# Reciprocals by GpSimd, moved small steps and a third tile of sign ranks in a fused attention and mixture-of-depths kernel

## The chip, the cores and the metric

The kernel runs on one core of one Trainium2 chip. The core has five engines that run at the same time, each with a queue of its own that it works through in order: TensorE (PE in the profile; its weight loads are shown apart as PEld), VectorE (DVE), ScalarE (ACT), GpSimd (POOL) and SyncE (SP), which issues most of the transfers. An engine waits for another by semaphores. The metric is the device time of one execution in microseconds, less is better, as the median of several executions.

## The reference

There are 8 batches, 8 heads, 576 rows of 64 channels. The first block is attention that keeps, in each row of scores, only the 32 largest:

```python
scores = scale * np.matmul(q, k.transpose(0, 1, 3, 2))
kth = np.partition(scores, -top_k, axis=-1)[..., -top_k:-top_k + 1]
scores = np.where(scores >= kth, scores, -1000000000.0)
scores = scores - np.max(scores, axis=-1, keepdims=True)
attn = np.exp(scores)
attn = attn / (np.sum(attn, axis=-1, keepdims=True) + 1e-09)
return np.matmul(attn, v)
```

Its heads are joined to rows of 512, and the second block, a mixture of depths, sends the 128 rows of each batch with the highest gate through a two-layer network:

```python
scores = np.einsum('bsd,d->bs', x, w_gate)
for b in range(B):
    top_idx = np.argpartition(-scores[b], capacity)[:capacity]
    xe = x[b, top_idx]
    ye = np.maximum(xe @ w1, 0.0) @ w2
    g = 1.0 / (1.0 + np.exp(-scores[b, top_idx]))
    out[b, top_idx] = x[b, top_idx] + g[:, None] * ye
```

## The kernel before

**Units.** A batch has five tiles of rows: four of 128 rows (tile numbers 0 to 3) and one of 64 (tile 4, `J`). A unit is one tile and two heads (for the last tile two heads of each half of the partitions), 18 units in a batch, 144 in all. The main loop (`for n in range(-1, N)`) is a software pipeline: in step n it multiplies the scores of unit n+1, searches the bound of unit n, finds the 32nd value of unit n-2, masks unit n-3 and forms the weighted values of unit n-4. `InOrder` keeps each engine's instructions in the order in which the program states them, so that the text of the loop is the order of every queue.

**One unit, engine by engine.**

- ScalarE copies the two score rows of 576 from PSUM (`keep`, tile `sc`).
- VectorE searches a bound (`find_bound`): for each of the two rows seven first maxima over a seventh of the row each (`cand`), then three rounds of eight maxima over the candidates, with the found ones struck out in between. The result is a bound that about the 24th largest score meets.
- ScalarE compares the row with that bound by a Sign (`part`, tiles `sides` in FP8 and the count `seen`), GpSimd multiplies the row by those signs and adds a short tail of fill values (`weigh_signs`, `fill`, tile `y`), and VectorE takes eight maxima of `y` (`find_kth`, tile `next`): the eighth is the 32nd largest score.
- ScalarE masks one row with it and GpSimd the other (`mask`, tile `less`).
- TensorE transposes the scores and adds the masks times a large negative number to them (`turn`, tile `ptr`). ScalarE takes the exponential (`pT`, `last`), TensorE multiplies by the values (`values`), with a column of ones that gives the sum of the weights.

**A finished tile.** After its last unit, ScalarE copies the products (`xs`) and the sums of weights (`keep_sums`, tile `sums`, eight numbers per row). One step later `normalise` calls `divide`: VectorE forms the eight reciprocals (`rden`), GpSimd multiplies. `normalise` is put on `vector_late`, a list that `find_bound` empties after the seven first maxima of its first row. Another step later VectorE forms the gates of the tile (`gates`, `dot`: a product with `wg` and a sum).

**The mixture of a batch** (`mixture`) is a generator whose pieces are spread over the steps of the next batch by the lists `mix_at` and `mix_at_of`. After the gates went through DRAM to a row on every partition (`gate_row`), the rank of each row of the batch is found tile by tile: for tiles 0 and 1 ScalarE adds up signs of gate differences (`weigh_gates`, put on `late`, which is emptied in each step ahead of the copies of the scores), for tiles 2, 3 and 4 VectorE counts larger gates (`choose`, on `vector_late`). GpSimd turns each rank into a row of the selection matrix `pick` (`choose_slot`, on `pool_late`, which is emptied after the bound of a step). TensorE then multiplies, and VectorE makes row numbers and gates of the products (`add_up`, on `after_kth`, emptied at the end of a step, behind the maxima of `y`). GpSimd fetches the chosen rows by an indirect transfer (`fetch_rows`), ScalarE forms exp(-gate), VectorE adds 1 and inverts (`squash`, on `vector_late`), TensorE runs the two layers, ScalarE scales the result by the gate, and GpSimd adds it to the output by another indirect transfer. For the last batch the same is written out by hand after the loop, with ranks counted in parts.

**A check at the end.** For each batch `keep_least` keeps the smallest 32nd value (`least`, a reduction by VectorE over 36 numbers a row) and a copy of the bounds. The last stage tests these, the counts and the sums; if a test fails, a slower general branch computes everything again. It isn't taken in these runs.

All instructions of the loop go through one recording line, so the profile gives L46 for them; they are told apart by the names of their tiles.

Of the kernel before, what the change touches and what calls it, by code (L numbers as in the profile page):

```python
# [11 lines left out]
ALU = mybir.AluOpType  # L12
FP32 = mybir.dt.float32
BF16 = mybir.dt.bfloat16
FP8 = mybir.dt.float8e4
# [34 lines left out]
def kernel(  # L50
# [11 lines left out]
    nc = tc.nc  # L62
    P = nc.NUM_PARTITIONS
    B, H, S, D = q.shape
# [55 lines left out]
    for i in range(2):  # L120
# [23 lines left out]
    bounded = const.tile([P, NS], FP32, name="bounded")  # L144
    sums = const.tile([P, B * NT, H], FP32, name="sums")
    nc.gpsimd.memset(sums, 1.0)

    MIDDLE = S - 2 * (TOP_K - 8) + 1
    steps_i = const.tile([P, 2, 8], I32, name="steps_i")
# [8 lines left out]
    nc.gpsimd.memset(ranks, 0.0)  # L158


    signs = const.tile([P, B - 1, 2], FP32, name="signs")
    places = const.tile([P, B, 7], FP32, name="places")
    nc.gpsimd.memset(places, 1.0)
    slot_signs = const.tile([P, CAP], FP32, name="slot_signs")
# [1 line left out]
        out=slot_signs,  # L166
# [57 lines left out]

    kept, values_bank = [], [None]

    after_kth = []

    def flush_copies():
        while copies_late:  # L230
# [2 lines left out]
    def flush():  # L233
        flush_copies()
        while late:
            late.pop(0)()
# [307 lines left out]
    def find_bound(sc, bound):  # L544

        cand = wkpool.tile([P, 2, 8 * PARTS], FP32, name="cand")
        best = [stats.tile([P, 2, 8], FP32, name=f"best{r}") for r in range(2)]
        best.append(bound)
        for i in range(2):

            if i == 1:
                flush_vector()
            for u in range(PARTS):
                if (i, u) == (1, 2) and amid_late:
                    amid_late.pop()()
                dve.max(
                    cand[:, i, 8 * u : 8 * u + 8],
                    sc[:, i, u * S // PARTS : (u + 1) * S // PARTS],
                )


        parts = cand.rearrange("p i (u e) -> p i u e", u=PARTS)
        for r, e in enumerate((3, 7, 8)):
            for i in range(2):
                dve.max(best[r][:, i, :], parts[:, i, :, 0:e])
            if r < 2:
                for i in range(2):
                    dve.match_replace(
                        parts[:, i, :, 0:e],
                        best[r][:, i, :],  # L570
                        parts[:, i, :, 0:e],
                        LOWEST,
                    )
# [163 lines left out]

    def divide(n, xs, x, den):
        rden = stats.tile([P, H], FP32, name="rden")
        dve.reciprocal(out=rden[0:n, :], in_=den)  # L740
        pool.tensor_tensor(
            x.rearrange("p (h d) -> p h d", h=H),
            xs[0:n, :, 0:D],
            rden[0:n, :].unsqueeze(2).to_broadcast([n, H, D]),
            ALU.mult,
        )
# [39 lines left out]
    def mixture(row0, pg, rank, exact=False, sign_sum=None):  # L786
# [36 lines left out]
        def choose_slot(t, n, slot=slot, rank=None):  # L823
            if rank is None:
                rank = rank_of[:, t : t + 1]
            pool.tensor_scalar(
                out=pick[0:n, t, :],
                in0=slot[0:n, :],
                scalar1=rank[0:n, :],
                scalar2=None,  # L830
                op0=ALU.is_equal,
            )

        for t in range(NT):
            yield
            n = R if t == J else P


            def weigh_gates(t=t):
                total = sign_sum[:, t : t + 1]  # L840
                act.activation(
                    pick.rearrange("p t c -> p (t c)")[:, 0:S],
                    gate_row,
                    AF.Sign,
                    bias=gate[:, t : t + 1],
                    scale=-1.0,
                    accum_out=total,
                )
                if t == 1:
                    for u in range(2):  # L850
                        pool_late.append(
                            lambda u=u: choose_slot(
                                u, P, slot_signs, sign_sum[:, u : u + 1]
                            )
                        )

            if t < 2 and not exact:
                late.append(weigh_gates)
                continue

            def choose(t=t, n=n):
                junk = modpool.tile([P, S], FP32, name="junk", tag="scratch")
                dve.tensor_scalar(
                    out=junk[0:n, :],
                    in0=gate_row[0:n, :],
                    scalar1=gate[0:n, t : t + 1],
                    scalar2=None,
                    op0=ALU.is_gt,
                    op1=ALU.add,
                    accum_out=rank[0:n, t : t + 1],  # L870
                )
                if exact:
                    break_ties(t, gate, gate_row, rank)

                pool_late.append(lambda: choose_slot(t, n))

            vector_late.append(choose)
# [16 lines left out]

        def add_up():
            add_parts(place, found)
            keep_rows(
                place,
                row_i,
                row0 if isinstance(row0, float) else row0[:, 0:1],  # L900
                float(done * S - 1),
            )
            dve.tensor_scalar_max(out=g, in0=place[:, 1:2], scalar1=-88.0)
            late.append(lambda: act.activation(g, g, AF.Exp, scale=-1.0))

        def squash():
            dve.tensor_scalar_add(out=g, in0=g, scalar1=1.0)
            dve.reciprocal(out=g, in_=g)

        kept.append(lambda: after_kth.append(add_up))  # L910
        if exact:
            for todo in (kept, after_kth):
                while todo:
                    todo.pop(0)()
        yield
# [15 lines left out]
        for fc in range(NFC):  # L931
            yield
            if fc == 1:
                vector_late.append(squash)
            if fc % 2 == 0:
                ps = ps_misc.tile([P, 2, CAP], FP32, name="h_ps", tag="misc")
            multiply_h(ps[:, fc % 2, :], fc, xeT)
            if fc % 2 == 1:
                copies_late.append(
                    lambda ps=ps, fc=fc: act.activation(  # L940
                        hT[:, fc - 1 : fc + 1, :], ps, AF.Relu
                    )
                )
# [34 lines left out]
    def add_parts(place, found):  # L978
        dve.tensor_reduce(
            out=place,  # L980
            in_=found[:, 0:6].rearrange("p (a e) -> p a e", e=3),
            axis=mybir.AxisListType.X,
            op=ALU.add,
        )

    def keep_rows(ps, row_i, row0, most):

        dve.tensor_scalar(
            out=row_i,
            in0=ps[:, 0:1],  # L990
            scalar1=row0,
            scalar2=most,
            op0=ALU.add,
            op1=ALU.min,
        )
# [178 lines left out]
    def keep_least(b, bound, kth):  # L1174
        at = 2 * per_batch * b
        late.append(
            lambda: act.copy(
                out=bounded[:, at : at + 2 * per_batch].rearrange("p (n i) -> p n i", i=2),
                in_=bound,
            )  # L1180
        )
        dve.tensor_reduce(
            out=least[:, b : b + 1], in_=kth, axis=mybir.AxisListType.XY, op=ALU.min
        )

    def mask_of(n, on=None):
# [346 lines left out]
        )  # L1533

    keep_least(B - 1, bounds.pop(B - 1)[:, :, :, 7], next8s.pop(B - 1)[:, :, :, 7])
    flush()
    low = modpool.tile([P, S], I32, name="low", tag="scratch")[:, 0:NS]
    dve.tensor_scalar(
# [88 lines left out]
    def general_weights(sc):  # L1627

        p = wkpool.tile([P, 2, S], FP32, name="p", tag="y")
        for i in range(2):  # L1630
            cur, tops = sc[:, i, :], []
            left = wkpool.tile([P, 2, S], FP32, name="left", tag="y")
            for r in range(TOP_K // 8):
                tops.append(stats.tile([P, 8], FP32, name=f"top{r}", bufs=2))
                nc.vector.max(tops[-1], cur)
                if r < TOP_K // 8 - 1:
                    nc.vector.match_replace(left[:, 0, :], tops[-1], cur, LOWEST)
                    cur = left[:, 0, :]
            shift = stats.tile([P, 1], FP32, name="shift", bufs=2)
            nc.vector.tensor_scalar_mul(shift, tops[0][:, 0:1], -scale)  # L1640
            e = wkpool.tile([P, S], FP32, name="e", tag="sides")
            nc.scalar.activation(
                e, sc[:, i, :], AF.Exp, bias=shift, scale=scale
            )
            nc.vector.scalar_tensor_tensor(
                out=p[:, i, :],
                in0=sc[:, i, :],
                scalar=tops[-1][:, 7:8],
                in1=e,
                op0=ALU.is_ge,  # L1650
                op1=ALU.mult,
            )
        return p
# [77 lines left out]
```

## Time and profile before

| | |
|---|---|
| median of 3 runs | 786.59 us (786.38 to 789.53) |
| the profiled execution | 788.9 us |
| its span, first to last instruction | 786.6 us |
| busy: TensorE, VectorE, ScalarE, GpSimd | 725.7, 756.7, 731.3, 692.4 us |
| main loop, units of steady batches | 92.29 us a batch of 18 units |
| VectorE busy from 50 to 700 us | 49.85 to 50.00 of every 50 us |
| ScalarE busy from 50 to 700 us | 47.11 to 49.94 of every 50 us |
| GpSimd busy from 50 to 700 us | 45.97 to 47.54 of every 50 us |
| mean granted TensorE clock | 0.996 of full speed |

In the profile a group of instructions stands in one row: line, engine, operation, what it writes and reads, shapes, count; then after the bar the busy time in microseconds and the mean of one in nanoseconds; then the idle time of the engine just before them, with the engine and tile whose semaphore ended most of it. In a list in order of time a row has the start and the length in microseconds, and in square brackets an idle time ahead of it. On VectorE and ScalarE the next instruction starts before the recorded end of the one before, so the lengths add up to more than the time that passes; the distance from start to start is what an instruction takes of its engine.

### The profile page before, as it was taken

To read this page: it belongs to the slowest core of one execution; us is meant where nothing else is said; L and a number is where in the kernel's file an instruction comes from. 1 tells how busy PE (TensorE), PEld (TensorE's weight loads), DVE (VectorE), ACT (ScalarE), POOL (GpSimd) and SP (SyncE) were. 2 spreads that over 40 slices of the span, in tenths; PEclk is the share of its full clock that TensorE was granted. 3 is DMA by queue.
4 is the path that set the end of the run, shared out by engine and by line. 5 is a ranking of instruction groups with operands and counts; after the bars stand their busy time and mean duration, and the time that the engine had idled before them with its cause. 6 is when DMAs were issued, how large, how long until landed. Compare 5 with 4: busy or idle time off the path is not lost. (4 is left out here: it accounts for less than half of the span.)

```text
span 786.6 us, 33176 instructions
## 1 busy us (share of the span) xinstructions
PE 725.7 (92%) x12535; PEld 550.5 (70%) x12535; DVE 756.7 (96%) x4602; ACT 731.3 (93%) x1535; POOL 692.4 (88%) x732
## 2 busy tenths in 40 slices
PE   8888888888999989999999999999899989999987
PEld 6766666666786668766786667866687658757756
DVE  7999999999999999999999999999999999999952
ACT  6999999999999999999999999999999999989730
POOL 3899999999999998999999999999999999999821
PEclk9999999999999999999999999999999999999899
DMA  8941215121151132321251221512233102101021
GB/s 168 293 105 39 48 56 111 30 55 30 62 118 35 38 94 54 76 57 42 70 110 31 56 43 63 114 26 50 65 77 82 30 15 70 25 15 17 2 75 31
DMA packets 121751, 50.69 MB, mean 64 GB/s; under 512 B 116016, under 2 KB 116016, under 8 KB 120560
## 3 DMA queue, kind: packets, MB, share of 16 engines
q1 hardware_dynamic: 118368, 43.94, 22.7%
q0 software_dynamic: 1744, 4.20, 3.0%
q8 instruction: 101, 1.65, 0.9%
q14 instruction: 66, 0.54, 0.2%
q10 hardware_dynamic: 1472, 0.36, 0.2%
HBM read 36.93 MB, written 11.55 MB: 62 GB/s over the span
## 5 line engine op out<-in xcount | busy, mean ns | idle before, releaser
L46 POOL TENSOR_TENSOR y<-sc,sides 128x576 f32<-128x576 f32 x288 | 349.8, 1237 | 24.8 <-ACT sides L46 23.3
L46 DVE MAX8 cand<-sc 128x8 f32<-128x82 f32 (+1 forms) x2016 | 313.1, 230 | 3.0 <-ACT sc L46 2.9
L46 POOL TENSOR_SCALAR less<-sc,next 128x576 bf16<-128x576 f32 x135 | 233.3, 1728 | 28.4 <-DVE next L46 23.8
L46 ACT ACTIVATE sides<-sc,bound 128x576 fp8e4<-128x576 f32 x288 | 230.9, 802 | 3.9 <-DVE bound L46 3.7
L46 PEld LDWEIGHTS av<-v,pT 128*64 128x64 f32 x4608 | 146.9, 138 | 87.2 <-ACT last L46 78.7
L46 DVE MAX8 next<-y 128x8 f32<-128x584 f32 x288 | 204.4, 751 | 0.0
L46 PE MATMUL av<-v,pT 128*64 128x65 f32 x4608 | 166.9, 225 | 35.0 <-ACT last L46 34.7
L46 PE MATMUL ps<-kT,qT 64*128 64x288 f32 (+1 forms) x1248 | 170.4, 422 | 2.9 <-ACT sc L46 2.1
L46 PEld LDWEIGHTS <-less 64*128 64x128 bf16 (+1 forms) x2448 | 161.2, 131 | 13.0 <-POOL less L46 10.0
L46 PE MATMUL ptr<-ident,sc 64*128 64x64 f32 x2272 | 161.5, 253 | 0.0
L46 ACT COPY sc<-ps 128x1152 f32<-128x1152 f32 x140 | 160.5, 1146 | 0.0
L46 ACT ACTIVATE pT<-ptr 128x1024 f32<-128x1024 f32 x142 | 147.3, 1037 | 10.1 <-PE ptr L46 9.3
L46 PEld LDWEIGHTS ptr<-ident,sc 64*128 64x128 f32 x2272 | 138.2, 137 | 23.8 <-issue 23.7
L46 PE MATMUL ptr<-out_of_reach,less 64*128 64x64 bf16 x2272 | 148.2, 190 | 6.3 <-POOL less L46 5.3
L46 ACT ACTIVATE less<-sc,next 128x576 bf16<-128x576 f32 x147 | 115.4, 789 | 0.0
L46 PEld LDWEIGHTS ps<-kT,qT 64*128 64x128 f32 (+1 forms) x1248 | 92.6, 176 | 22.6 <-ACT sc L46 5.1
L46 DVE MATCH_REPLACE8 cand<-best,cand 128x21 f32<-128x21 f32 (+1 forms) x576 | 99.0, 180 | 0.0
L46 DVE MAX8 best<-cand 128x8 f32<-128x21 f32 (+1 forms) x576 | 91.0, 191 | 0.0
L46 ACT ACTIVATION_READ_ACCUMULATOR sides<-sc,bound 128x1 f32 x288 | 63.6, 221 | 0.0
L46 PE MATMUL h_ps<-xeT,w 128*128 128x128 f32 x464 | 61.9, 278 | 0.0
L46 PEld LDWEIGHTS av<-ident,sc 128*128 128x128 f32 x144 | 20.0, 139 | 55.9 <-issue 40.9
L46 PE MATMUL av<-vpair,last 128*64 128x130 f32 x576 | 56.9, 276 | 0.0
(167 smaller groups left out, 916.2 us busy)
## 6 DMA issues: line engine op xcount, KB each, us to landing
v<-in_v_dram SPq DMA_DIRECT2D x64, 128.0 KB, 4.0
out_dram<-x SPq DMA_DIRECT2D x8, 1024.0 KB, 3.9
rows<-in_k_dram SPq DMA_DIRECT2D x56, 128.0 KB, 2.9
rows<-in_q_dram SPq DMA_DIRECT2D x56, 128.0 KB, 3.1
w<-in_moe_w_dram SPq DMA_DIRECT2D x2, 2048.0 KB
gate_row<-row_dram SPq DMA_DIRECT2D x7, 288.0 KB, 4.6
last<-in_q_dram SPq DMA_DIRECT2D x8, 128.0 KB, 3.5
vpair<-in_v_dram SPq DMA_DIRECT2D x16, 64.0 KB, 5.1
```

The costliest lines, as they stand in the source:

```text
L46: return lambda *a, **kw: self._tc.keep_in_program_order(fn(*a, **kw))
```

## The change

The change has three parts and two consequences.

1. `divide` and `squash` form their reciprocals on GpSimd, as a power with exponent -1. A new constant tile `minus_one` holds the exponents. The addition of 1 in `squash` goes along, and `squash` is put on `pool_late`.
2. A new list `after_max` is emptied by `find_bound` after each first maximum, so in effect after the first one of the next unit. On it go the reduction of `least` and the part of `add_up` that follows its sum: `use_place`, with the row number, the limited gate and the request for its exponential.
3. `SIGNED` = 3 tiles, not two, have their ranks added up from signs by ScalarE. The signs are written to a tile of their own in FP8 (`gate_signs`) and not to `pick`, and each tile's slots are chosen as soon as its sum is there, not those of tiles 0 and 1 together.

In the general branch, a work tile takes another buffer. The last stage's own reciprocals, written out there, stay on VectorE.

```diff
+    minus_one = const.tile([P, H], FP32, name="minus_one")
+    nc.gpsimd.memset(minus_one, -1.0)
...
-    signs = const.tile([P, B - 1, 2], FP32, name="signs")
+    SIGNED = 3
+    signs = const.tile([P, B - 1, SIGNED], FP32, name="signs")
...
-    after_kth = []
+    after_kth, after_max = [], []
...
                 dve.max(
                     cand[:, i, 8 * u : 8 * u + 8],
                     sc[:, i, u * S // PARTS : (u + 1) * S // PARTS],
                 )
+                while after_max:
+                    after_max.pop(0)()
...
     def divide(n, xs, x, den):
         rden = stats.tile([P, H], FP32, name="rden")
-        dve.reciprocal(out=rden[0:n, :], in_=den)
+        pool.tensor_tensor(rden[0:n, :], den, minus_one[0:n, :], ALU.pow)
         pool.tensor_tensor(
             x.rearrange("p (h d) -> p h d", h=H),
             xs[0:n, :, 0:D],
...
             def weigh_gates(t=t):
                 total = sign_sum[:, t : t + 1]
+                unread = modpool.tile([P, S], FP8, name="gate_signs")
                 act.activation(
-                    pick.rearrange("p t c -> p (t c)")[:, 0:S],
+                    unread,
                     gate_row,
                     AF.Sign,
                     bias=gate[:, t : t + 1],
                     scale=-1.0,
                     accum_out=total,
+                    saturate=False,
                 )
-                if t == 1:
-                    for u in range(2):
-                        pool_late.append(
-                            lambda u=u: choose_slot(
-                                u, P, slot_signs, sign_sum[:, u : u + 1]
-                            )
-                        )
-
-            if t < 2 and not exact:
+                pool_late.append(lambda: choose_slot(t, P, slot_signs, total))
+
+            if t < SIGNED and not exact:
                 late.append(weigh_gates)
                 continue
...
         def add_up():
             add_parts(place, found)
+            after_max.append(use_place)
+
+        def use_place():
             keep_rows(
...
         def squash():
-            dve.tensor_scalar_add(out=g, in0=g, scalar1=1.0)
-            dve.reciprocal(out=g, in_=g)
+            pool.tensor_scalar(
+                out=g, in0=g, scalar1=1.0, scalar2=None, op0=ALU.add
+            )
+            pool.tensor_tensor(g, g, minus_one[:, 0:1], ALU.pow)

         kept.append(lambda: after_kth.append(add_up))
         if exact:
-            for todo in (kept, after_kth):
+            for todo in (kept, after_kth, after_max):
                 while todo:
                     todo.pop(0)()
...
             if fc == 1:
-                vector_late.append(squash)
+                pool_late.append(squash)
...
-        dve.tensor_reduce(
-            out=least[:, b : b + 1], in_=kth, axis=mybir.AxisListType.XY, op=ALU.min
+        after_max.append(
+            lambda: dve.tensor_reduce(
+                out=least[:, b : b + 1], in_=kth, axis=mybir.AxisListType.XY, op=ALU.min
+            )
         )
...
     keep_least(B - 1, bounds.pop(B - 1)[:, :, :, 7], next8s.pop(B - 1)[:, :, :, 7])
+    after_max.pop()()
     flush()
```

More of the change, by code (lines that the diff above doesn't have):

```diff
@@ L1640, in general_weights @@
             nc.vector.tensor_scalar_mul(shift, tops[0][:, 0:1], -scale)
-            e = wkpool.tile([P, S], FP32, name="e", tag="sides")
+            e = modpool.tile([P, S], FP32, name="e", tag="scratch")
             nc.scalar.activation(
```

## The prediction

> **What bounds the kernel now.** I read the page's busy table first, then the costliest groups, then one steady batch, then single stretches of each engine in order of time.
>
> ```profile
> PE 725.7 (92%) x12535; PEld 550.5 (70%) x12535; DVE 756.7 (96%) x4602; ACT 731.3 (93%) x1535; POOL 692.4 (88%) x732
> 381.69:473.98 92.29, 88.75 (x1549) 66.78 (x1549) 92.19 (x569) 91.27 (x194) 86.46 (x89) 1.00 0.27 63
> ```
>
> The second line is busy time in one batch of 18 units, from a unit's first maximum to the same one a batch later: PE, PEld, DVE, ACT, POOL. The batch before and the one after have the same period, 92.3 us. VectorE is never idle, ScalarE is idle 1.0 us, GpSimd 5.8 us. So VectorE sets the period, and ScalarE stands about 1% behind it: that second fact decides how much of a cut on VectorE can be cashed. What VectorE does beside its maxima:
>
> ```profile
> L46 DVE TENSOR_SCALAR_CACHE_REDUCE junk<-gate_row,gate 128x576 f32<-128x576 f32 x14 | 11.2, 799 | 0.0
> L46 DVE RECIPROCAL rden<-sums 128x8 f32<-128x8 f32 x32 | 6.0, 188 | 2.4 <-ACT sums L46 2.4
> L46 DVE RECIPROCAL g<-g 128x1 f32<-128x1 f32 x8 | 1.3, 164 | 0.3
> ```
>
> Durations overstate what an instruction costs its engine, because the next one starts before it ends. VectorE in order of time:
>
> ```profile
> 471.65 1.42 DVE L46 MAX8 next<-y 128x8 f32<-128x584 f32 x2
> 473.10 0.22 DVE L46 TENSOR_REDUCE least<-next 128x1 f32<-128x36 f32 x1
> 473.24 1.11 DVE L46 MAX8 cand<-sc 128x8 f32<-128x82 f32 x7
> 474.26 0.18 DVE L46 RECIPROCAL rden<-sums 128x8 f32<-128x8 f32 x1
> 474.37 0.34 DVE L46 MAX8 cand<-sc 128x8 f32<-128x82 f32 x2
> ```
>
> The reciprocal occupies 474.37 - 474.26 = 0.10 us (unrounded 0.101), not 0.188. The reduction starts 0.03 us after the maxima end instead of some 0.085 us before: it reads what they have just written, and VectorE stands still 0.12 us for it. The rank of one tile:
>
> ```profile
> 443.11 0.80 DVE L46 TENSOR_SCALAR_CACHE_REDUCE junk<-gate_row,gate 128x576 f32<-128x576 f32 x1
> 443.82 0.08 DVE L46 DVE_READ_ACCUMULATOR junk<-gate_row,gate 128x1 f32 x1
> 443.82 1.12 DVE L46 MAX8 cand<-sc 128x8 f32<-128x82 f32 x7
> ```
>
> occupies 0.72 us. The same rank as a sum of signs on ScalarE:
>
> ```profile
> 422.66 0.83 ACT L46 ACTIVATE pick<-gate_row,gate 128x576 bf16<-128x576 f32 x1
> 423.33 0.26 ACT L46 ACTIVATION_READ_ACCUMULATOR pick<-gate_row,gate 128x1 f32 x1
> 423.42 0.44 ACT L46 ACTIVATE qT<-ps 128x256 f32<-128x256 f32 x1
> ```
>
> occupies 423.42 - 422.66 = 0.76 us. On GpSimd, where a tile is normalised:
>
> ```profile
> 453.30 1.72 POOL L46 TENSOR_SCALAR less<-sc,next 128x576 bf16<-128x576 f32 x1 [0.65 <-DVE next L46]
> 455.00 1.03 POOL L46 TENSOR_TENSOR x<-xs,rden 128x512 f32<-128x512 f32 x1
> 456.00 2.39 POOL L46 TENSOR_TENSOR y<-sc,sides 128x576 f32<-128x576 f32 x2
> ```
>
> The multiply follows the mask at once; it doesn't wait for VectorE's reciprocal.
>
> **What the Trainium skill says.** "Perfetto Trace Analysis", GPSIMD Engine Instruction: GpSimd spans are unreliable, take start-to-start spacing. I do; the trace agrees where it matters (the mask: 1.72 long, 1.70 spaced). "ScalarE: Activation LUTs", What ACT_TABLE_LOAD costs: 280 ns + 0.833 ns an element with a pointer bias, back-to-back overlap about 93 ns. For 576 elements that is an estimate of 760 and 667; an unqueued Sign here takes 767, spaced 667. "GPSIMD Engine Reference", 3.1: about 2.6 cycles an element for two inputs, 1.25 us for 576 by its 1.2 GHz; the trace has 1237 ns. No page prices a power on GpSimd.
>
> **The change, part by part** (spacing, not duration).
> VectorE loses, over the run:
> - 38 reciprocals of the sums in the loop at 0.10 us: 3.8. (Of the 40 rows one is in the last stage through the same helper, one stays.)
> - Seven ranks of tile 2 at 0.72: 5.0.
> - Seven squashes (add, then a reciprocal that waits for it: 0.174 + 0.080): 1.8.
> - Seven reductions of the thresholds, moved behind the first maximum of the next unit: the stall of 0.12 each, 0.8. The instruction stays.
> - The row number and gate moved likewise: row_i started 0.034 us after the sum ended and now follows a maximum, 0.12 each, 0.8.
> Together 12.3 us, 1.76 per batch in steady state. The moved steps issue no DMA. What waits for them: the fetch of the rows by GpSimd comes after a 1.7 us mask that itself waits for the maxima, so a row number about 0.5 us later is covered (uncovered: 0.5 us seven times, on GpSimd); the Exp of the gate slips one unit, and its reader comes units later.
>
> ScalarE gains seven Signs at 0.76: 5.3. Each stands in its queue ahead of the copies of the turned rows and of the next scores, and so of everything VectorE reads next. The FP8 target instead of pick takes away a write that pick's readers had to release; ScalarE never waits visibly for that, so nothing.
>
> GpSimd gains 39 powers of 8 wide, seven adds and seven powers 1 wide. Slots chosen stay at 35; they come one by one. The mask or multiply that follows in GpSimd's queue waits behind each. A small operation that waits for its predecessor is spaced 0.27 us here (the splits of the gates, 200 ns each), the lower bound of a power. No row bounds it from above. A 576-element multiply spends about 1.8 ns an element; if a power is 20 to 40 of those, eight are 0.3 to 0.6 us: estimate 0.55 for the whole spacing, and I let it run to 1.5. New work per batch at 0.55: 5 x 0.55 + 0.27 + 0.4 = 3.4 us.
>
> **Why VectorE's 12.3 us won't all arrive.** I set each start-to-start spacing of ScalarE in the batch above against the shortest tenth of its kind. The excess that ends with another engine is about 1.6 us of 92.29: 0.7 waiting for the bounds from VectorE, 0.8 for turned scores from TensorE, 0.1 other. Give it 0.76 and take away every wait: 92.29 - 1.6 + 0.76 = 91.45. VectorE would need 92.29 - 1.76 = 90.53. ScalarE becomes the bound. The wait for the bounds disappears by itself (VectorE is early); the wait for TensorE only in part, since TensorE itself waits for ScalarE's last weights and for GpSimd's masks. I take 1.25 of 1.6 as removable: gain 0.5 per batch.
>
> The margin that VectorE can run ahead first: it starts a unit 1.3 to 3.8 us after that unit's scores are copied, 2.19 in the unit right after the new Sign. So:
> - up to the first wait for scores: 2.19 - 0.76 = 1.4 us
> - four further batches at 0.5: 2.0
> - the last batch, after the last such wait, where ScalarE has slack (busy 42.9 of the 50 us from 700 on): VectorE's own savings, 1.5
> - last stage: the last normalisation starts at 751.44 after sums ending 751.12; the power takes 0.3 us more than the reciprocal, and the values of the last unit queue behind the gates: -0.3. The two counts that stood behind VectorE's 2.4 us wait for those sums run earlier, but nothing waits for them there.
> Sum 4.6 us.
>
> The profiled execution took 788.9 us, with a span of 786.6, so 2.3 us lie around it; they don't change. The median of the runs is 786.59. I take the difference off the median: 782.0 us.
>
> **Rivals.**
> - *VectorE stays the bound.* All of 12.3: 774.3 us. For it: VectorE has no idle, and parts of ScalarE's spacing may shrink when less queues. Against: the 1 us of idle. 0.17.
> - *ScalarE sets the pace*, 782.0, itself 779 to 784.5. 0.45.
> - *The gain is absorbed.* GpSimd's mask is ready between 0.5 us before and 0.9 us after TensorE starts that unit's turns, and ScalarE takes the result as little as 0.07 us later. Powers ahead of masks make those later by their length in the units where GpSimd has no idle (30 us at a time), so ScalarE's waits stay: gain 0 to 0.1 per batch, 785.5. That the change doesn't do what it says belongs here. 0.18.
> - *GpSimd becomes the bound* (slower). Its spacings, taken the same way, fill 85.3 of 92.29 us. With powers of p in both widths it needs 85.3 + 6p + 0.27; above p = 1.1 us that exceeds today's period. At 1.4: 94.0, 1.7 a batch, seven batches: 798 us. 0.20.
>
> **How the numbers follow.** A measurement of this kernel tells about 0.5% from no change, so 782.66 and 790.5 are the edges. Faster: 0.17 and four fifths of 0.45, 0.53. Same: the other fifth and 0.18, 0.27. Slower 0.20. The range runs from the full VectorE gain, 774, to 790, which holds the absorbed case and a power just above its threshold; most of the slower case is left out.
>
> **What would show it.** VectorE: waits for the score copies on the first maximum, 0 to 1 us in the units after the new Sign, where there were none; its busy time 12 to 17 us less. ScalarE: its waits for the bounds gone, its busy share of a steady batch over 99%. GpSimd: the row of the power, spaced under 1 us, and the idle before its masks down from 28.4 us. A batch period of 91.8. Wrong if VectorE still shows no wait at a period of 90.5 (first rival), if powers take over 1.1 us (last), or if TensorE's waits for masks grow while the period stays at 92.

## The result, and the profile after

The changed kernel takes 858.84 us, against 788.01 for the kernel before in the same measurement (medians of five executions each): 1.0895 times, interval 1.0878 to 1.0912. The prediction was 782.0. The profiled execution took 858.87 us, with a span of 857.0.

First the busy table of the kernel after, and busy time in one steady batch of it (us from and to, length, then PE, PEld, DVE, ACT and POOL busy, and at the end TensorE's granted clock, DMA share and GB/s):

```profile
PE 747.3 (87%) x12535; PEld 562.4 (66%) x12535; DVE 782.7 (91%) x4535; ACT 740.2 (86%) x1549; POOL 780.4 (91%) x786
410.00:512.28 102.28, 92.13 (x1553) 68.59 (x1549) 95.59 (x559) 92.66 (x195) 97.98 (x96) 0.97 0.26 57
```

A batch takes 102.28 us and not 92.29. No engine is busy all the time any more: GpSimd is idle for 4.3 us, the least of all, VectorE for 6.7, ScalarE for 9.6. GpSimd's busy time grew by 11.5 us a batch, more than the period. VectorE's grew by 3.4, although work was taken from it. The groups with different shapes kept apart show both surprises, the power and the gates' product:

```profile
L46 POOL TENSOR_TENSOR rden<-sums,minus_one 128x8 f32<-128x8 f32 x32 | 53.5, 1672 | 3.3 <-ACT sums L46 3.3
...
L46 POOL TENSOR_TENSOR g<-g,minus_one 128x1 f32<-128x1 f32 x7 | 4.3, 621 | 0.6
...
L46 DVE CUSTOM_DVE_ANT_0 prod<-x,wg 128x512 f32<-128x512 f32 x32 | 40.0, 1251 | 6.6 <-POOL x L46 6.5
L46 DVE CUSTOM_DVE_ANT_0 prod<-x,wg 64x512 f32<-64x512 f32 x8 | 20.8, 2598 | 8.7 <-POOL x L46 8.6
```

The power takes 1.67 us; I had put it at 0.55. The product for the gates, which wasn't touched, takes 1.25 us at 128 rows and 2.60 us at 64. In the kernel before it took 0.84 and 0.69:

```profile
L46 DVE CUSTOM_DVE_ANT_0 prod<-x,wg 128x512 f32<-128x512 f32 x32 | 27.0, 844 | 0.1
...
L46 DVE CUSTOM_DVE_ANT_0 prod<-x,wg 64x512 f32<-64x512 f32 x8 | 5.5, 693 | 0.0
```

The waits, longest first (columns: who waits for whom, us in total, times, longest):

```profile
PEld L46 <- POOL less L46: 68.4, 46, 2.6
ACT pT L46 <- PE ptr L46: 65.4, 66, 2.7
...
DVE cand L46 <- ACT sc L46: 29.9, 38, 2.1
...
POOL y L46 <- ACT sides L46: 26.9, 30, 10.1
...
DVE prod L46 <- POOL x L46: 15.1, 24, 1.7
```

In the kernel before, the first two were:

```profile
PEld L46 <- POOL less L46: 10.0, 27, 1.0
ACT pT L46 <- PE ptr L46: 9.3, 17, 1.6
```

VectorE waited 2.9 us for score copies there, GpSimd 23.3 us for signs, and the list has no wait of the product for rows. So there is a chain of waits behind GpSimd: TensorE waits for GpSimd's masks, ScalarE for TensorE's turned scores, VectorE for ScalarE's score copies. The link that would close it to a ring, GpSimd's wait for ScalarE's signs, hardly grew, and one wait of 10 us at the start is in both of its numbers. GpSimd's idle time ahead of its masks went from 28.4 us to nothing. One unit with a finished tile shows the chain. GpSimd in order of time:

```profile
426.27 1.74 POOL L46 TENSOR_SCALAR less<-sc,next 128x576 bf16<-128x576 f32 x1
427.98 1.66 POOL L46 TENSOR_TENSOR rden<-sums,minus_one 64x8 f32<-64x8 f32 x1
429.72 1.04 POOL L46 TENSOR_TENSOR x<-xs,rden 64x512 f32<-64x512 f32 x1
430.72 2.40 POOL L46 TENSOR_TENSOR y<-sc,sides 128x576 f32<-128x576 f32 x2
433.08 0.66 POOL L46 TENSOR_TENSOR y<-steps,seen 128x16 f32<-128x16 f32 x1
433.73 1.72 POOL L46 TENSOR_SCALAR less<-sc,next 128x576 bf16<-128x576 f32 x1
```

From one mask to the next lie 433.73 - 426.27 = 7.46 us; in the steady batch before, most masks lay 4.8 to 5.5 us apart. TensorE, ScalarE and VectorE at that place:

```profile
432.83 0.25 PE L46 MATMUL ptr<-ident,sc 64*128 64x64 f32 x2
435.50 0.24 PE L46 MATMUL ptr<-out_of_reach,less 64*128 64x64 bf16 x2 [2.42 <-POOL less L46]
```

```profile
436.42 1.02 ACT L46 ACTIVATE pT<-ptr 128x1024 f32<-128x1024 f32 x1 [2.56 <-PE ptr L46]
```

```profile
428.01 1.39 DVE L46 MAX8 cand<-sc 128x8 f32<-128x82 f32 x9
430.79 2.87 DVE L46 CUSTOM_DVE_ANT_0 prod<-x,wg 64x512 f32<-64x512 f32 x1 [1.39 <-POOL x L46]
```

VectorE waits 1.39 us for the normalised rows (which is the multiply that follows the power), and then its product lasts 2.87 us, through both multiplications of `y` by GpSimd. I add up start-to-start spacings on VectorE between the first and the last maximum of `y`, a stretch that went from 727.4 to 798.7 us, +71.3: the product takes 28.3 more, its wait for rows 15.6, waits for scores 31.3, waits for `y` 6.4. Less the 12.3 us taken off, that is +69.3.

TensorE's clock changed as well. Between 50 and 750 us of the span the kernel after has fourteen stretches of 3.4 us in which the granted clock is half, two in a steady batch; the kernel before has one such stretch, of 6.8 us, at 742 us. One of the fourteen begins where TensorE goes on above (the number after GpSimd's busy time is the clock):

```profile
435.50:438.90 3.40, 3.40 (x25) 2.30 (x26) 3.40 (x18) 1.78 (x3) 3.40 (x4) 0.50 0.57 84
```

TensorE's transposes there took 0.35 us against 0.25 before the wait. Each of the fourteen begins within 1.2 us of the end of an idle time of TensorE of 1.5 to 2.5 us. Other idle times of that length have none behind them, and what decides isn't shown here.

### The profile page after: what moved, and what is told of

Read it like the earlier page. It is cut to its first block, busy times and chain, and to the rows that moved or that the text cites. A ratio compares the mean times of both kernels' runs of the same rounds, so it can differ in the third digit from the quotient of the medians.

```text
span 857.0 us, 33088 instructions
## 1 busy us (share of the span) xinstructions
PE 747.3 (87%) x12535; PEld 562.4 (66%) x12535; DVE 782.7 (91%) x4535; ACT 740.2 (86%) x1549; POOL 780.4 (91%) x786
## 5 line engine op out<-in xcount | busy, mean ns | idle before, releaser
L46 POOL TENSOR_TENSOR y<-sc,sides 128x576 f32<-128x576 f32 x288 | 364.6, 1290 | 29.6 <-ACT sides L46 26.9
L46 ACT ACTIVATE sides<-sc,bound 128x576 fp8e4<-128x576 f32 x288 | 226.5, 787 | 0.1
L46 PE MATMUL ptr<-out_of_reach,less 64*128 64x64 bf16 x2272 | 150.5, 190 | 62.7 <-POOL less L46 61.7
L46 ACT ACTIVATE pT<-ptr 128x1024 f32<-128x1024 f32 x142 | 145.3, 1023 | 66.2 <-PE ptr L46 65.4
L46 PE MATMUL ps<-kT,qT 64*128 64x288 f32 (+1 forms) x1248 | 183.3, 445 | 3.4 <-ACT sc L46 3.4
L46 PE MATMUL ptr<-ident,sc 64*128 64x64 f32 x2272 | 164.6, 253 | 0.0
L46 PEld LDWEIGHTS ps<-kT,qT 64*128 64x128 f32 (+1 forms) x1248 | 99.1, 185 | 24.3 <-ACT sc L46 5.3
L46 DVE CUSTOM_DVE_ANT_0 prod<-x,wg 128x512 f32<-128x512 f32 (+1 forms) x40 | 60.8, 1520 | 15.2 <-POOL x L46 15.1
L46 POOL TENSOR_TENSOR rden<-sums,minus_one 128x8 f32<-128x8 f32 (+1 forms) x39 | 65.2, 1671 | 3.3 <-ACT sums L46 3.3
L46 PEld LDWEIGHTS av<-ident,sc 128*128 128x128 f32 x144 | 20.6, 143 | 60.5 <-issue 39.6
```

The lines of the kernel that those rows point to most:

```text
L46: return lambda *a, **kw: self._tc.keep_in_program_order(fn(*a, **kw))
```

## The experiments

Four theories were to be told apart. A: the length of the power. B: its place in GpSimd's queue. C: ScalarE's third Sign. Later D (the gates' product standing still beside GpSimd takes VectorE's savings) and S (ScalarE sets the pace, the prediction's own reading). Below, "product" is the sum of the 40 products' lengths, in us, and "waits" are VectorE's waits for score copies between the first and the last maximum of `y`, taken from start-to-start spacings.

**A short operation in the power's place.**

```diff
-        pool.tensor_tensor(rden[0:n, :], den, minus_one[0:n, :], ALU.pow)
+        pool.tensor_tensor(rden[0:n, :], den, minus_one[0:n, :], ALU.mult)
```

> The changed kernel with one word changed: GpSimd multiplies the sums by -1 where it took their power, so that the tiles, the queues and the waits are the same and only the operation's length differs. It leaves the reciprocal out of the attention's result. Theory A (the power's length of 1.67 us is the cause: GpSimd's queue gets 1.4 us later per tile, and the collisions of the gates' product follow from that): the operation takes 0.2 to 0.3 us, the time falls to 776 to 786, near the forecast of 782 for a short power, and the gates' product goes back under 1.0 us on average. Theory B (the place of the reciprocal in GpSimd's queue is the cause: the row is ready later and the gates' product meets GpSimd's multiplications at any length): 800 to 830, with the product still over 1.2 us. Theory C (ScalarE's third Sign is the cause): over 840.

794.6 us, 1.0076 (1.0053 to 1.0099) of the kernel before. So 64 of the 71 us go with the power's length, but none of the ranges was met: with an operation of 0.20 us the kernel is still slightly slower than before, where A expected a gain. B's sign, products over 1.2 us, is there, but not its time. The products say why:

```profile
L46 DVE CUSTOM_DVE_ANT_0 prod<-x,wg 128x512 f32<-128x512 f32 x32 | 40.3, 1259 | 0.2 <-POOL x L46 0.2
L46 DVE CUSTOM_DVE_ANT_0 prod<-x,wg 64x512 f32<-64x512 f32 x8 | 10.6, 1330 | 0.0
```

At 128 rows they are as long as with the power, at 64 rows half as long, and they no longer wait for their rows. In order of time, GpSimd and then VectorE:

```profile
400.91 2.39 POOL L46 TENSOR_TENSOR y<-sc,sides 128x576 f32<-128x576 f32 x2
403.27 0.66 POOL L46 TENSOR_TENSOR y<-steps,seen 128x16 f32<-128x16 f32 x1
```

```profile
402.19 1.66 DVE L46 CUSTOM_DVE_ANT_0 prod<-x,wg 64x512 f32<-64x512 f32 x1
```

The multiplications end at 403.30, and the product ends 0.55 us later, a little less than its own 0.67 us, as do nearly all products in this run that meet them. So it stood still until they were nearly done; GpSimd's next operation, 0.22 us otherwise, took 0.66 while the product ran. This is theory D.

**The reciprocals of the sums back on VectorE, the rest as changed.**

```diff
-        pool.tensor_tensor(rden[0:n, :], den, minus_one[0:n, :], ALU.pow)
+        dve.reciprocal(out=rden[0:n, :], in_=den)
```

> The changed kernel with the reciprocals of the sums back on VectorE; the gates' reciprocal stays a power on GpSimd, and the moved steps and the third tile of signs stay. Theory A and theory B (the power, by its length or its place): 778 to 786, the rest of the change a gain of 0 to 1%. Theory C (ScalarE's third Sign): over 840, nearly as slow as the changed kernel.

785.75 us, 0.9977 (0.9965 to 0.9989), in the range of A and B. C falls: ScalarE's Sign is still there. The rest of the change is worth 1.8 us, although it takes 8.4 us off VectorE; the products grew from 32.5 to 39.6.

**The powers of the sums alone, in the kernel before.**

```diff
-        dve.reciprocal(out=rden[0:n, :], in_=den)
+        pool.tensor_tensor(rden[0:n, :], den, minus_one[0:n, :], ALU.pow)
...
```

> The kernel before with one edit: the reciprocals of the sums as powers on GpSimd (and the general branch's work tile in the other buffer, for room). Theory A and theory B: 850 to 865, all of the loss. Theory C: under 800.

850.78 us, 1.0754 (1.0673 to 1.0836), in the first range. 63 of the 71 us come with these 39 instructions without anything else of the change. One of the four executions took 839.84 us, at a mean granted clock of 0.987; the other three took 850.56 to 852.18, at 0.969 to 0.971. So the same instructions take 11 to 12 us less where the clock is higher.

**The gates one unit later.**

```diff
-        gating = normalised
+        gating = waiting
+        waiting = normalised
...
```

> The changed kernel with the gates of each tile formed one unit later on VectorE (and the first pieces of the mixture one unit later for that), so that the gates' product needn't wait for GpSimd's normalised rows. If the product's wait and its meeting with GpSimd's multiplications (some 43 us of VectorE in the changed kernel) are what the power costs: 810 to 830, and no wait of the product for GpSimd. If GpSimd's own queue, five powers of 1.7 us a batch, sets the pace in any case, by the masks that TensorE waits for: 845 to 862, with VectorE waiting as much for scores as it no longer waits for rows.

847.37 us, 1.0757 (1.0727 to 1.0788), in the second range, but not by the wait that I named for it. The product's wait for rows went from 15.6 us to nothing and waits for scores fell too, from 31.8 to 15.2; instead waits for `y`, which GpSimd makes, rose from 6.6 to 27.4. Most of what was gained at one place was lost at another, with GpSimd behind both. This kernel also has eight stretches of half clock and not fourteen, which by the price worked out below is some 7 of the 11.5 us that it gains. (In its seventh batch the chosen rows are used before their fetch; that changes values and not the work.)

**The product with one input.** In the kernel before, in the changed kernel with the short operation, and in the changed kernel with its powers:

```diff
-        dve.tensor_tensor_reduce(
-            out=prod[0:n, 0:HD], in0=x, in1=wg[0:n, :], scale=1.0, scalar=0.0,
-            op0=ALU.mult, op1=ALU.add, accum_out=g,
-        )
+        dve.tensor_scalar(
+            out=prod[0:n, 0:HD], in0=x, scalar1=1.0, scalar2=None,
+            op0=ALU.mult, op1=ALU.add, accum_out=g,
+        )
```

> The kernel before with the one-input product (it leaves the gates' weights out): the control. Before, 40 products take 32.5 us, of which some 5 are standing still. Theory D and theory S: 783 to 789, since the one-input form has 0.05 us more spacing each.

780.62 us, 0.9901 (0.9886 to 0.9915), below the range. The products fell from 32.5 to 26.7 us, and the one-input form isn't longer than a two-input product that doesn't stand still (both are spaced about 0.6 us): already before the change, standing still cost a little more than I had put down.

> The changed kernel with a multiplication by -1 in place of the power, as in e1_mult, and with the gates' product reading one tensor, the rows, and not the weights beside them (a multiplication by 1 with the same sum over the row). It leaves out the reciprocal and the gates' weights. Theory D (VectorE's savings go to the gates' product, which stands still while GpSimd runs a multiplication with two inputs): the product stays under 0.8 us everywhere, VectorE gets its 12.3 us, 772 to 780. Theory S (ScalarE sets the pace, as in the prediction): the product is short as well, but VectorE waits for score copies instead, over 12 us in all, and the time is 782 to 788.

781.19 us, 0.9913 (0.9899 to 0.9927), between the two ranges. The one-input product in the kernel with the short operation (those of 64 rows take 0.66 us):

```profile
L46 DVE TENSOR_SCALAR_CACHE_REDUCE prod<-x 128x512 f32<-128x512 f32 x32 | 21.4, 669 | 0.2 <-POOL x L46 0.2
```

It never stands still (0.66 to 0.69 us over all 40), so D's mechanism is confirmed; against e1_mult, 13.4 us are gained. But VectorE, which has 12.3 us less to do than in the control, is no faster than it. The waits, and then busy time in one steady batch of this kernel and of the control, e6_before_one_input:

```profile
DVE cand L46 <- ACT sc L46: 11.9, 26, 2.1
```

```profile
370.67:462.93 92.26, 88.31 (x1555) 66.73 (x1553) 90.59 (x560) 91.75 (x195) 88.46 (x96) 1.00 0.27 63
373.70:465.37 91.67, 88.46 (x1553) 66.75 (x1551) 91.57 (x569) 91.11 (x193) 86.54 (x89) 1.00 0.26 63
```

Waits for scores went from 0.6 us in the control to 12.1, nearly the whole saving, and ScalarE, the fourth number after the length, is busy for 99.4% of its batch (first line). So S decides, once the collisions are gone. The period is 92.26 us, 0.6 more than the control's: with the third tile of signs ScalarE holds the kernel at the period that it had before the change.

> The changed kernel, powers and all, with the one-input product (it leaves the gates' weights out). If the products' standing still (some 28 us more than before) is most of what the powers cost: 815 to 832. If GpSimd's queue with its powers sets the pace by itself: 840 to 856, and VectorE waits for scores instead, over 50 us.

834.81 us, 1.0585 (1.0570 to 1.0601), between the two ranges and nearer to the first, with waits for scores under the 50 us that I named for the second. Of the loss of 70.8 us, 834.81 - 780.62 = 54.2 stay when no product can stand still. Some 17 us go with the collisions, and by the price worked out below about half of them come by the clock, for this kernel has seven stretches of half clock and not fourteen. What sets the pace now is GpSimd; one steady batch:

```profile
405.01:503.96 98.95, 90.72 (x1549) 68.11 (x1549) 91.52 (x559) 92.46 (x196) 95.70 (x96) 0.98 0.24 59
```

It is idle for 3.25 us, VectorE and ScalarE for twice as long. And its busy time is what the sum gives: 86.46 before, five powers of 1.67 and 0.8 for the gates make 95.6.

**The signs and the moved steps without any power.**

```diff
-            pool.tensor_tensor(g, g, minus_one[:, 0:1], ALU.pow)
+            dve.reciprocal(out=g, in_=g)
```

and likewise the reciprocals of the sums, and the addition ahead of the gates' reciprocal, with `squash` on `vector_late`.

> The moved steps and the third tile of signs alone, both reciprocals on VectorE as before. VectorE saves 5.0 + 0.8 + 0.8 = 6.6 us. Theory D: most of it goes to the product, 783 to 788, the products 36 to 45 us in all and VectorE's waits for scores as before, under 7 us. Theory S: 784 to 788 too, but by waits for scores over 8 us.

785.64 us, 0.9971 (0.9956 to 0.9986), in both ranges. Products 36.4, waits 0.9: that is theory D. Of 6.6 us taken off VectorE, 3.9 go to products. It can't be told from e2_recip_back, so the gates' power, 7 x 0.62 us, costs nothing that was measured.

**How a power's length counts.**

```diff
-        pool.tensor_tensor(rden[0:n, :], den, minus_one[0:n, :], ALU.pow)
+        pool.tensor_tensor(
+            rden[0:n, 0 : H // 2], den[:, 0 : H // 2], minus_one[0:n, 0 : H // 2], ALU.pow
+        )
...
```

> The changed kernel with the power taken over four of the eight heads; the other four are multiplied by 1 (their reciprocal is left out). The gates' power, one wide, takes 0.58 us and the sums' power, eight wide, 1.67, so 0.156 us an element and 1.05 us for four. Theory L (a power's length lands whole in the period, because GpSimd's mask, TensorE, ScalarE and the gates' product follow each other in every unit with a finished tile): on the line from e1_mult (0.20 us, 794.6) to the changed kernel (1.67 us, 858.8), 831, that is 824 to 838. Theory of the prediction (GpSimd's idle takes up a power to 1.1 us): 792 to 806.

```profile
L46 POOL TENSOR_TENSOR half_rden<-sums,minus_one 128x4 f32<-128x4 f32 x32 | 33.4, 1043 | 3.3 <-ACT sums L46 3.3
```

823.6 us, 1.0441 (1.0408 to 1.0474): 0.4 us below L's range, and far above the other theory's.

| GpSimd's operation per tile | length | median us |
|---|---|---|
| none (e2_recip_back) | | 785.75 |
| multiplication, 8 wide (e1_mult) | 0.20 | 794.6 |
| power, 4 wide (e9_power_four) | 1.04 | 823.6 |
| power, 8 wide (the changed kernel) | 1.67 | 858.84 |

For 39 instructions the second step adds 39 x 0.84 = 32.8 us of GpSimd time and 29.0 us of kernel time, the third 24.6 and 35.2. No step is free, but the first one goes with the collisions: with the one-input product the short operation left the kernel at 781.19 us, against 780.62 in the control.

The third step costs more than the time that it adds. Part of this is TensorE's clock. In the trace of e9_power_four lowered and full clock alternate from batch to batch; two batches in a row:

```profile
301.23:399.28 98.05, 90.65 (x1555) 68.31 (x1553) 95.34 (x559) 92.36 (x196) 94.78 (x96) 0.98 0.26 59
399.28:496.14 96.86, 89.13 (x1556) 66.93 (x1553) 95.32 (x559) 92.36 (x196) 94.75 (x96) 1.00 0.25 60
```

The work of the other engines is the same, and the batch with one stretch of half clock takes 1.2 us more; the next two batches repeat it. At 1.2 us each, my estimate is that the fourteen stretches of the changed kernel cost 17 of its 71 us. e9_power_four has four and e1_mult none, so some 12 of the third step's 35.2 us and 5 of the second's 29.0 are the clock's. No kernel here without the powers of the sums has more than one such stretch before its end, so I take them as a consequence of the powers.

**Where the product stands best.** In the kernel before, two short maxima later; then with the small steps moved; then in e8_signs_moved behind the first round over the candidates:

```diff
-                if (i, u) == (1, 2) and amid_late:
+                if (i, u) == (1, 4) and amid_late:
```

> The kernel before with the gates' product two of the short maxima later, 0.29 us, so that it starts at least 0.57 us after GpSimd's mask where it started 0.28 to 0.35 us after it. Theory D (the product stands still beside GpSimd, in the first half microsecond of a mask too): 40 products take 27 to 29 us, not 32.5, and the time falls by 3 to 5 us to 783 to 785. Rival: the length of those products has another cause: no change, 787 to 789.

> e10_product_later with the small steps behind the next first maximum as in the changed kernel; no power and no third tile of signs. VectorE saves 1.6 us more. Theory D and theory S, since ScalarE gets no new work and has some 1.6 us a batch to give: 781 to 784, faster than both kernels. If small steps hide anyway: the same as e10_product_later.

> e8_signs_moved with the gates' product behind the first round of maxima over the candidates, about 1.3 us later, where GpSimd is at its mask in most of those units. Theory D: the products take 27 to 31 us and not 36.4, and the time is 780 to 784, with waits for scores growing since ScalarE has the third Sign. Rival: the product meets the next multiplication instead: 785 to 790, products over 36 us.

| | ratio, interval | median us | product | waits |
|---|---|---|---|---|
| before, same measurement | 1 | 788.19 | 32.5 | 0.5 |
| e10_product_later | 0.9951, 0.9932 to 0.9969 | 783.98 | 30.3 | 0.6 |
| e11_moved_later | 0.9956, 0.9943 to 0.9970 | 785.13 | 31.4 | 0.6 |
| e12_signs_round | 0.9996, 0.9983 to 1.0010 | 787.73 | 37.9 | 2.8 |

The first is faster than both kernels, by one changed number; its time is in D's range, its products at 30.3 us just above theirs. Not all of the 4.2 us is the product's: about half of the executions of the kernel before have a mean clock of 0.996 and take 790.3 us, and those at 0.999 take 786.18, against 783.72 for the first kernel at the same clock. What it avoids is a product that meets a mask in its first half microsecond. In a steady batch it avoids one of two; the other, some 0.2 us into a mask, stays at 1.05 to 1.07 us. The kernel before, GpSimd and then VectorE:

```profile
437.43 1.73 POOL L46 TENSOR_SCALAR less<-sc,next 128x576 bf16<-128x576 f32 x1
```

```profile
437.71 1.01 DVE L46 CUSTOM_DVE_ANT_0 prod<-x,wg 128x512 f32<-128x512 f32 x1
```

The second missed its range (781 to 784). Its gain comes from the same place: between the first and the last maximum of `y` it took 724.4 us against 725.1, so the moved steps bring at most some 0.7 of their 1.6 us, and the medians don't tell the two apart. The third fell to its rival: later there, the product met other multiplications in the early batches.

## Why the prediction was wrong

**What bounds the kernel: half right.** VectorE without idle and ScalarE 1% behind it were read rightly, and that ScalarE stops VectorE's savings is what e5_mult_one_input shows. But the period of that stop was too low: 91.45 without any wait and 91.8 expected, 92.26 measured. The gain of 0.5 us a batch that the forecast of 782 rests on wasn't there even with a short operation and no collision, and the steady batches of e2_recip_back (92.6) and e8_signs_moved (92.3) were no shorter than before. There are two stops, and the nearer one was missed. With the real product VectorE did not wait for scores in e1_mult or e8_signs_moved (1.1 and 0.9 us); its savings went to products that stood still.

**VectorE's 12.3 us: about right.** In e5_mult_one_input waits for scores rose by 11.5 us over the control while the stretch from the first to the last maximum of `y` grew by 0.7, so some 10.8 us of saved work are found again. Costing its instructions by start-to-start spacing held.

**The power at 0.55 us: the first step that failed.** It took 1.67 us, above even the 1.5 that I let it run to. I scaled from a 576-element multiplication by a factor of 20 to 40 that nothing in the trace gave. The trace of before had no row for a power, and so the upper bound of the slower case should not have been drawn as near to the guess.

**GpSimd's idle as room: the second step, and the larger one.** What came is the last rival, "GpSimd becomes the bound", to which I gave 0.20; its sign, powers over 1.1 us, is there too. But its sum was also too small. With the measured price it gives 85.3 + 5 x 1.74 + 0.9 for the gates = 94.9 us a batch, 2.6 more than before, over seven batches about 805 us. The measured period is 102.28, of which GpSimd is busy for 97.98. In busy time the same sum gives 86.46 + 5 x 1.67 + 0.8 = 95.6, and e7_after_one_input measures 95.70. Two terms are missing:

- 2.3 us a batch by which GpSimd's other operations became longer; in e7_after_one_input they are down to 0.1, so they belong to the product that collides with them (the multiplications of `y` went from 1237 to 1290 ns on average).
- 4.3 us of idle that stayed. The sum let the powers fill all of GpSimd's idle. Before, 3.4 of its 5.8 us a batch lay ahead of masks, and those were filled. The rest, ahead of multiplications that wait for signs and ahead of small steps, was not, and it is larger where the clock is lowered: in e9_power_four GpSimd is idle for 2.1 us in a batch at full clock and for 3.3 us in one with a lowered stretch.

The threshold of 1.1 us fell with these terms: at 1.04 us (e9_power_four) the period was already 96.9 to 98.1. The rival in which the gain is absorbed named the path from a late mask to TensorE and ScalarE, but let it take back the gain and no more. Whether a power at another place in GpSimd's queue would have cost less was not tried.

**The gates' product: a missing term.** I noted that the multiply of the rows "doesn't wait for VectorE's reciprocal" and went no further. The one who waits for these rows, VectorE's product, was left out of the sum, and so was what its place beside GpSimd's operations does to its length. Its rows 844 against 693 ns in the profile before were the sign: an instruction of one length that varies with what another engine does. The Trainium skill has the rule, which I didn't draw on: "SBUF — State Buffer", Who interferes with whom, says that a VectorE instruction with two inputs in SBUF contends with a GpSimd instruction that reads SBUF, and that one with at most one such input doesn't, outside the two-port modes. The runs agree (0.67 to 2.88 us with two inputs in the kernel after, 0.66 to 0.69 with one), but not with the page's statement, under Terms, that the lock is held for the whole instruction. Beside a mask of 1.73 us the product above ended 1.29 us after the mask's start, and so did every product of the kernel before that started in the first 0.6 us of a mask. With 0.67 us of work of its own, it seems to have begun at about 0.6 us into the mask; its true start isn't shown.

**The last stage.** From the last maximum of `y` to the end of the span it took 40.0 us before and 39.3 after. This doesn't test the loss of 0.3 us: the profiled execution of before has its stretch of half clock there, and e1_mult and e2_recip_back, without one, took 37.5 and 37.7.

## What to carry to other kernels

Before an operation goes to an engine with idle time, ask what that idle waits for: here only the part ahead of the masks could be filled, 3.4 of 5.8 us a batch, and what is left decides when the engine becomes the bound. Count with it what the new work does to the length of others. Cost an unknown operation by a measurement of its own, since scaling from another operation bounded nothing here. And where one row's length varies under equal shapes, find what it collides with first: moving that one instruction by two short maxima was worth more (783.98 us) than eight microseconds of work taken from the busiest engine (785.75).

## What the hardware showed that I had not expected

- A power on GpSimd takes 0.58 us (median) for one element a row, 1.04 for four and 1.67 for eight: about 0.43 us and 0.156 us an element, an estimate from the three. A multiplication of the same eight takes 0.20.
- VectorE's two-input product stood still through two multiplications by GpSimd in a row, 2.87 us for 0.67 us of work. It didn't slip in between them. GpSimd's next operation grew from 0.22 to 0.66 us beside it.
- TensorE's granted clock fell to half for 3.4 us at a time, fourteen times, beside idle times of 1.5 to 2.5 us. Two batches of one trace with equal work differ by 1.2 us with one such stretch.
